# Handing the loads of a memory-bound attention kernel from SyncE's hardware queue to Pool's software queue, with 8 rows asked for per packet

## The chip, the cores and the metric

The kernel runs on one core of one Trainium2 chip. The metric is device time in microseconds (us). Times are medians of several executions. "Landing" is the moment at which the last of 16 semaphore writes of a load has happened, by the packet records of the trace. A "row" is the part of a load in one partition. The profile calls SyncE's queue `hardware_dynamic` and Pool's `software_dynamic`; here they are the hardware and the software queue, and the "hardware descriptors" and "software descriptors" are loads by the one and by the other. The experiments ran in three sessions, each on another chip and each with the kernel before in the same rounds.

## The reference

One query token attends over a cache of 16384 keys and values in 32 heads; the result is projected and mixed, by a gate, with a small gated MLP of the same token.

```
q      = (x @ wq).reshape(1, 1, 32, 128)                    # x: 512
scores = einsum('bhqd,bhkd->bhqk', q, k_cache) * 128**-0.5  # k_cache: 32 x 16384 x 128, bf16
o      = einsum('bhqk,bhkd->bhqd', softmax(scores), v_cache)
a      = o.reshape(1, 1, 4096) @ wo
b      = gMLP(x)                                            # small
out    = g * a + (1 - g) * b
```

The two caches are 268 MB of the 279.58 MB that must be read, and every byte is used once.

## The kernel before

Heads are worked in 16 pairs. A pair has one load of keys (K_i) and one of values (V_i), 8.4 MB each: 128 partitions of 64 KB. In the packet records a load is 16 chains of 8 rows of 64 KB, each chain ended by one semaphore write: so each of the 16 DMA engines carries 8 rows of every load. Three buffers of 64 KB per partition take the loads in turn, in the order K_0, K_1, V_0, K_2, V_1, K_3, ... A load waits until the load three places before it has been used. SyncE issues all loads; Pool waits for each landing and hands it on to DVE or PE.

```python
k_at = [max(2 * i - 1, 0) for i in range(NP)]            # place of K_i in the order of loads
v_at = [min(2 * i + 2, 2 * NP - 1) for i in range(NP)]
# ... (user[n]: the event after which the buffer of load n is free)
for n, kind, i in loads:
    wait = [user[n - 3]] if n >= 3 else [w_free] if buf[n % 3] is setup else []
    src = (k_src if kind == "k" else v_src)[i]
    cuts, sems = (0, KP), [(ld_k if kind == "k" else ld_v)[i % 2]]
    # ... (the last pair's loads are cut into pieces)
    for a, b, done in zip(cuts[:-1], cuts[1:], sems):
        sp.op(lambda e, a=a, b=b, n=n, src=src: e.dma_start(
            out=buf[n % 3][:, a * Dh:b * Dh], in_=src[:, a * Dh:b * Dh]),
            wait=wait if a == 0 else (), inc=(done, 16))
# ... (five pieces of wo, the same way)

def hand(e, loaded, to, n):
    e.wait_ge(loaded, 16).then_inc(to, n)
    e.nop().then_inc(loaded, -16)
# ... (pool_pairs: a hand() for every load, in order)
```

K_1 (load 1) waits for nothing and is queued right behind K_0. V_0 (load 2) needs the buffer that holds the weights of the setup; it waits for `w_free`, the end of the gMLP. DVE multiplies the keys by the query, PE sums the products and ACT takes the exponentials, after which a key buffer is free. V_1 is load 4: it waits until K_1 (load 1) has been used.

The softmax here doesn't subtract the row's maximum and nothing guards it: scores larger than these inputs give would overflow.

Of the kernel before, what the change touches and what calls it, by code (L numbers as in the profile page):

```python
# [13 lines left out]
Dh = 128  # L14
H = 32
NP = H // 2
D = 512
# [9 lines left out]
KP = Sk // 64  # L27
# [7 lines left out]
WG = 8  # L35
NT = NG // TG
ZB = F // 4
K_CUTS = (0, 128, 256)
V_CUTS = (0, 160, 224, 256)
WO_CUTS = (0, 16, 24, 28, 31, 32)  # L40
WIDE = 24
# [126 lines left out]
def gated_mix_kernel(nc, A_x, A_k_cache, A_v_cache, A_wq, A_wo, B_x, B_w_in, B_w_sp, B_b_sp,  # L168
                     B_w_out, gate_w, out):
    def sb(name, shape, dt):  # L170
# [3 lines left out]
    buf = [bufs[:, b * ROW:(b + 1) * ROW] for b in range(3)]  # L174
# [42 lines left out]
    wo_at = 2 * NP  # L217
# [5 lines left out]
    wo = buf[wo_at % 3]  # L223
# [5 lines left out]
    sem = nc.alloc_semaphore  # L229
# [1 line left out]
    half = sem("half")  # L231
    ld_x, ld_g, ld_q, ld_w, ld_u, st_out = (
        sem(n) for n in ("ld_x", "ld_g", "ld_q", "ld_w", "ld_u", "st_out"))
    ld_k = [sem(f"ld_k{b}") for b in range(2)]
    ld_v = [sem(f"ld_v{b}") for b in range(2)]
    ld_kh = [sem(f"ld_kh{b}") for b in range(len(K_CUTS) - 1)]
    ld_vp = [sem(f"ld_vp{b}") for b in range(len(V_CUTS) - 1)]
    ld_o = [sem(f"ld_o{b}") for b in range(len(WO_CUTS) - 1)]
    k_s, v_s, mul_s, red_s, sum_s, exp_s, sl_s, pv_s, drn_s, zer_s, wo_s = (
        sem(n) for n in ("k_s", "v_s", "mul_s", "red_s", "sum_s", "exp_s", "sl_s", "pv_s", "drn_s",  # L240
                         "zer_s", "wo_s"))
# [4 lines left out]
    pool, sp, pe, dve, act = (Queue(nc, e, n) for e, n in (  # L246
        (nc.gpsimd, "pool"), (nc.sync, "sp"), (nc.tensor, "pe"), (nc.vector, "dve"),
        (nc.scalar, "act")))
# [6 lines left out]
    def value(e, reg, top):  # L255
# [5 lines left out]
        out=ident[:, :], in_=ident[:, :], compare_op=ALU.not_equal, fill=1.0, base=0,  # L261
        pattern=[[-1, P]], channel_multiplier=1))
    for t in [L_sb, p_t, zero]:
# [5 lines left out]
           inc=(ld_x, 16))  # L269
    act.op(lambda e: e.dma_start(out=gw_row[:, :], in_=gate_w.rearrange("(a d) -> a d", a=1)),  # L270
           inc=(ld_g, 16))
    act.op(lambda e: e.dma_start(out=wb_row[:, 0:1], in_=B_w_sp), inc=(ld_g, 16))
    act.op(lambda e: e.dma_start(out=wb_row[:, 1:2], in_=B_b_sp.rearrange("(a d) -> a d", a=1)),
           inc=(ld_g, 16))
    sp.op(lambda e: e.dma_start(out=wq, in_=A_wq.rearrange("(p c) n -> p (c n)", c=DC)),
          inc=(ld_q, 16))
    sp.op(lambda e: e.dma_start(out=w_in, in_=B_w_in.rearrange("(p c) f -> p (c f)", c=DC)),
          inc=(ld_w, 16))
    sp.op(lambda e: e.dma_start(out=w_out, in_=B_w_out.rearrange("(p k) n -> p (k n)", k=FhC)),
          inc=(ld_u, 16))  # L280

    for c in range(DC):
# [9 lines left out]
        out=sel[:, :].rearrange("h (i x) -> h i x", x=P + 1)[:, :, 0:P:4],  # L292
        in_=ident[0:H, 0:H].unsqueeze(1).broadcast_to([H, 4, H])), wait=[const_ok, ident_ok],
        mark=True)
    dve.op(lambda e: e.tensor_reduce(
        out=pick[:, :].rearrange("p (r s) -> p s r", r=4),
        in_=ident[:, :].rearrange("p (g x) -> p x g", x=32)[:, 0:8, :]
# [10 lines left out]
           wait=[g_ok], mark=True)  # L308
# [52 lines left out]
    for h in range(2):  # L361
        zh = ps_all[:, 6 * h * 512:(6 * h + 2) * 512].rearrange("p (b x) -> p b x", b=2)[:, :, 0:ZB]
        dve.op(lambda e, h=h, zh=zh: e.tensor_tensor(  # L363
            out=zm[:, 2 * h * ZB:2 * (h + 1) * ZB].rearrange("p (b m k) -> p b m k", b=2, k=FhC),
# [5 lines left out]
        out=z[:, :].rearrange("p (e k) -> p e k", e=2),  # L370
        in_=zm.rearrange("p (e m k) -> p e k m", e=2, k=FhC), axis=AX.X, op=ALU.add))
    dve.chain(lambda e: e.scalar_tensor_tensor(
        out=zt[:, :], in0=z[:, :], scalar=0.044715, in1=z[:, :], op0=ALU.mult, op1=ALU.mult))
    zt_ok = dve.chain(lambda e: e.scalar_tensor_tensor(
        out=zt[:, :], in0=zt[:, :], scalar=1.0, in1=z[:, :], op0=ALU.add, op1=ALU.mult))
# [5 lines left out]
           wait=[sg_ok], mark=True)  # L381
# [11 lines left out]
        out=var[:, :], in0=mv[:, 0:1], scalar=mv[:, 0:1], in1=mv[:, 1:2], op0=ALU.mult,  # L393
# [9 lines left out]
        out=u[:, :], in0=z2n[:, :], scalar=gm_sb[:, 0:1], in1=z[:, 0:FhC], op0=ALU.mult,  # L403
        op1=ALU.mult))
    u_ok = (dve.sem, dve.n)
# [6 lines left out]
        out=ps_all[:, 2 * 512:6 * 512].rearrange("p (n s x) -> p n s x", n=2, s=2)[:, :, 0, :],  # L412
        in_=zero[:, :].unsqueeze(1).broadcast_to([P, 2, 512])))
# [188 lines left out]
    user = {}  # L602
    for i in range(NP):
        user[k_at[i]], user[v_at[i]] = used_k[i], used_v[i]
    loads = sorted([(n, "k", i) for i, n in enumerate(k_at)]
                   + [(n, "v", i) for i, n in enumerate(v_at)])
    for n, kind, i in loads:
        wait = [user[n - 3]] if n >= 3 else [w_free] if buf[n % 3] is setup else []
        src = (k_src if kind == "k" else v_src)[i]
        cuts, sems = (0, KP), [(ld_k if kind == "k" else ld_v)[i % 2]]  # L610
        if i == NP - 1:
            cuts, sems = (K_CUTS, ld_kh) if kind == "k" else (V_CUTS, ld_vp)
        for a, b, done in zip(cuts[:-1], cuts[1:], sems):
            sp.op(lambda e, a=a, b=b, n=n, src=src: e.dma_start(
                out=buf[n % 3][:, a * Dh:b * Dh], in_=src[:, a * Dh:b * Dh]),
                wait=wait if a == 0 else (), inc=(done, 16))
    wo_src = A_wo.rearrange("(p k) n -> p (k n)", k=H)
    for j, (a, b) in enumerate(zip(WO_CUTS[:-1], WO_CUTS[1:])):
        sp.op(lambda e, a=a, b=b: e.dma_start(out=wo[:, a * D:b * D], in_=wo_src[:, a * D:b * D]),  # L619
              wait=[user[wo_at - 3]] if a == 0 else (), inc=(ld_o[j], 16))  # L620

    def hand(e, loaded, to, n):
        e.wait_ge(loaded, 16).then_inc(to, n)
        e.nop().then_inc(loaded, -16)

    def pool_pairs(e):
        hand(e, ld_k[0], k_s, 2)
        with e.Fori(0, NP // 2 - 1):
            hand(e, ld_k[1], k_s, 2)
            hand(e, ld_v[0], v_s, NT)  # L630
            hand(e, ld_k[0], k_s, 2)
            hand(e, ld_v[1], v_s, NT)
        for j in range(len(ld_kh)):
            hand(e, ld_kh[j], k_s, 1)
        hand(e, ld_v[0], v_s, NT)
        for j, (a, b) in enumerate(zip(V_CUTS[:-1], V_CUTS[1:])):
            hand(e, ld_vp[j], v_s, (b - a) * NT // KP)

    pool.raw(pool_pairs)

    dve.op(lambda e: e.reciprocal(out=rl[:, :], in_=l_ps[:, 0:H]), wait=[(sl_s, 1)], mark=True)  # L641
    dve.chain(lambda e: e.tensor_scalar(out=rl[:, :], in0=rl[:, :], scalar1=g_sb[:, 0:1],
# [12 lines left out]
    o2_ok = dve.op(lambda e: e.tensor_copy(out=o2[:, :], in_=l_ps[:, P:P + H]), wait=[o2p_ok],  # L655
                   mark=True)

    def pool_wo(e):
        e.wait_ge(*d_zero)
        e.wait_ge(*o2_ok)  # L660
        for j, (a, b) in enumerate(zip(WO_CUTS[:-1], WO_CUTS[1:])):
            if a < WIDE:
                hand(e, ld_o[j], wo_s, (min(b, WIDE) - a) // WG)

    pool.raw(pool_wo)

    def pe_wide(e):
        va, pa = (counter(e, n, 0) for n in ("wa", "oa"))
# [33 lines left out]
    for q in (dve, act):  # L702
        mine = range(NC)[:NC // 2] if q is dve else range(NC)[NC // 2:]
        for s in mine:
            ok = q.op(lambda e, s=s, copy=(q is act): (e.copy if copy else e.tensor_copy)(  # L705
                out=res[0:1, s * DQ:(s + 1) * DQ], in_=a_ps[32 * s:32 * s + 1, 0:DQ]),
                wait=[y_ok] if s in mine[:1] else (), mark=(s == mine[-1]))
        sp.raw(lambda e, ok=ok: e.wait_ge(*ok))
    sp.op(lambda e: e.dma_start(out=out.rearrange("a b d -> (a b) d"), in_=res[:, :]),
          inc=(st_out, 16))  # L710
# [19 lines left out]
def build(inputs):  # L730
    import numpy as _np
    import concourse.bacc as _bacc
    from concourse import mybir as _mybir

    nc = _bacc.Bacc("TRN2", target_bir_lowering=False, num_devices=1, dynamic_dma_scratch_size=4096)
    arrays, args = {}, []
    for name in _INS:
        a = _np.ascontiguousarray(inputs[name])
        if a.dtype.kind in "iu":
            a = a.astype(_np.int64)  # L740
        arrays[f"in_{name}_dram"] = a
        args.append(nc.dram_tensor(f"in_{name}_dram", a.shape, _mybir.dt.from_np(a.dtype), kind="ExternalInput").ap())
    for i, (shape, dtype) in enumerate(_OUTS):
        dt = _mybir.dt.from_np(_np.dtype(dtype))
        args.append(nc.dram_tensor(f"out_{i}_dram", shape, dt, kind="ExternalOutput").ap())
    gated_mix_kernel(nc, *args)
    return nc, arrays
# [9 lines left out]
```

## Time and profile before

| | before |
|---|---|
| median time | 651.7 us (20 runs, 651.5 to 652.7) |
| span in the profile | 650.0 us |
| DMA, mean over the span | 430 GB/s |
| PE, DVE busy | 66%, 52% |
| mean step from landing to landing, steady state | 19.350 us |

These are lines of the profile's page of the kernel before. `DMA` gives the busy share of the 16 DMA engines in tenths for 40 equal slices, `GB/s` what they moved; the line starting `DMA 4%` is the chain that ended last.

```profile
span 650.0 us, 7735 instructions
DMA  9999999999999999999999989999999999999998
DMA packets 6203, 279.60 MB, mean 430 GB/s; under 512 B 695, under 2 KB 826, under 8 KB 1210
q1 hardware_dynamic: 6194, 279.58, 99.6%
DMA 4%; PE 0%; SPq 0%; issue 0%; DVE 0%; ACT 0%; ACTq 0%
```

The loads bound the kernel from end to end: the packets of the hardware queue take 99.6% of the span of the 16 engines. How little is left is told by the packet records: the fastest rows of 64 KB start 2414 ns apart on an engine, and 99% of the rows that follow another without a gap (under 2500 ns from start to start) start 2414 to 2429 ns after it. An estimate from the 2414 ns, if all 279.58 MB moved at that rate on 16 engines, is 643.6 us for the bytes.

The timeline of SyncE before shows when (start and duration of the issuing instruction):

```profile
2.03 1.04 SPq L614 DMA_DIRECT2D bufs<-in_A_k_cache_dram  x2
35.15 0.33 SPq L614 DMA_DIRECT2D bufs<-in_A_v_cache_dram  x1
66.40 0.33 SPq L614 DMA_DIRECT2D bufs<-in_A_k_cache_dram  x1
91.86 0.33 SPq L614 DMA_DIRECT2D bufs<-in_A_v_cache_dram  x1
101.32 0.33 SPq L614 DMA_DIRECT2D bufs<-in_A_k_cache_dram  x1
```

In order they are K_0 and K_1, V_0, K_2, V_1, K_3. By the packet records K_2 ends at 95.05 us on the first engine and 95.59 on the last. The lead, from V_1's issue to the end of K_2 on the first engine, is 3.2 us. Compute decides when V_1 can be issued, and in the timeline of DVE compute begins when K_0 has landed (37.56 us) and has been handed on:

```profile
31.06 0.23 DVE L402 SCALAR_TENSOR_TENSOR u<-z2n,gm_sb,z 128x7 bf16<-128x7 f32 x1
38.32 8.76 DVE L557 TENSOR_TENSOR bufs<-bufs,qb  x2 [7.03 <-DVEq L84]
```

The first line is the event `u_ok` (31.3 us), which the change uses. The second is the first product with K_0.

### The profile page before, as it was taken

How to read it: one execution, taken by the hardware profiler on the slowest of the kernel's cores; microseconds unless marked ns; L12 is line 12 of the kernel's file. 1: busy time of each engine (PE TensorE's matmuls, PEld its weight loads, DVE VectorE, ACT ScalarE, POOL GpSimd, SP SyncE). 2: the span in 40 equal slices, each digit the busy share in tenths (PEclk: the TensorE clock that was granted, in tenths of full speed). 3: DMA queues.
4: the chain of work that ended last, by engine and by line, in shares of the span. 5: the costliest groups of instructions: out<-in, count | busy, mean ns of one | idle time of the engine just before them, and what ended most of it. 6: DMA issues, size and time to landing. Idle time of an engine off the chain costs nothing. (4 is left out here: it accounts for less than half of the span.)

```text
span 650.0 us, 7735 instructions
## 1 busy us (share of the span) xinstructions
PE 428.8 (66%) x2464; PEld 44.2 (7%) x1304; DVE 336.2 (52%) x159; ACT 45.8 (7%) x112; POOL 2.1 (0%) x10
## 2 busy tenths in 40 slices
PE   0547687847487584747857476684747757478767
PEld 0000000000101000010000101000010100001012
DVE  3457848256380745618265470835629075465600
ACT  2200100000001000010100001000010100001011
POOL 1000000000000000000000000000000000000000
PEclk9958788969779686987968798686988968798999
DMA  9999999999999999999999989999999999999998
GB/s 385 466 415 452 452 391 448 452 432 407 452 452 399 440 452 444 395 452 452 407 432 452 452 387 452 452 407 432 452 452 391 448 452 423 415 425 478 390 428 345
DMA packets 6203, 279.60 MB, mean 430 GB/s; under 512 B 695, under 2 KB 826, under 8 KB 1210
## 3 DMA queue, kind: packets, MB, share of 16 engines
q1 hardware_dynamic: 6194, 279.58, 99.6%
q8 instruction: 1, 0.02, 0.0%
q10 hardware_dynamic: 8, 0.00, 0.0%
HBM read 279.58 MB, written 0.00 MB: 430 GB/s over the span
## 5 line engine op out<-in xcount | busy, mean ns | idle before, releaser
L557 DVE TENSOR_TENSOR bufs<-bufs,qb x64 | 281.5, 4419 | 167.7 <-DVEq L84 167.7
L88 PE MATMUL ps_all<-bufs,ident 128*128 x960 | 267.6, 436 | 0.0
L475 PE MATMUL ps_all<-bufs,ident 128*128 x64 | 28.6, 446 | 148.2 <-PEq L84 148.2
L101 PE MATMUL ps_all<-bufs,p_t 128*8 x1024 | 79.1, 384 | 30.5 <-PEq L84 19.9
L542 DVE TENSOR_REDUCE s_sb<-ps_all 128x64 f32<-128x512 f32 x64 | 44.1, 689 | 97.8 <-DVEq L84 97.8
L88 PE MATMUL ps_all<-zero,ident 128*8 128x512 bf16 (+1 forms) x165 | 57.9, 383 | 0.0
L569 ACT ACTIVATE p_t<-s_sb 64x256 f32 (+1 forms) x32 | 13.3, 414 | 433.4 <-ACTq L84 433.0
L475 PEld LDWEIGHTS ps_all<-bufs,ident 128*128 128x128 bf16 x64 | 6.3, 99 | 367.8 <-issue 367.8
L101 PEld LDWEIGHTS ps_all<-bufs,p_t 128*8 x1024 | 17.9, 82 | 163.6 <-issue 163.2
L510 PE MATMUL ps_all<-pick,d_sb 128*128 128x2 f32 x128 | 16.8, 253 | 16.5 <-PEq L84 16.5
L510 PEld LDWEIGHTS ps_all<-pick,d_sb 128*128 128x128 f32 x128 | 15.5, 191 | 34.7 <-issue 34.7
L578 ACT COPY d_sb<-ps_all 128x512 f32<-128x512 f32 x16 | 9.4, 585 | 104.3 <-ACTq L84 104.3
L583 ACT CAST ps_all<-zero 128x512 f32<-128x512 bf16 x15 | 8.8, 589 | 1.7
L644 DVE TENSOR_TENSOR o_sb<-ps_all,rl 128x32 bf16<-128x32 f32 x1 | 0.2, 191 | 11.5 <-PE ps_all L510 11.5
L641 DVE RECIPROCAL rl<-ps_all 128x32 f32<-128x32 f32 x1 | 0.4, 357 | 11.1 <-PE ps_all L531 11.1
L363 DVE TENSOR_TENSOR bufs<-ps_all,ident 128x896 f32<-128x896 f32 x2 | 2.1, 1086 | 7.6 <-PE ps_all L88 7.6
L569 ACT ACTIVATION_READ_ACCUMULATOR p_t<-s_sb (+1 forms) x32 | 5.9, 185 | 0.0
L305 PE MATMUL ps_all<-xgw,const-float32-1.0 1*128 1x3 f32 x2 | 0.6, 360 | 8.0 <-DVE xgw L302 8.0
L101 PE MATMUL ps_all<-bufs,u 128*1 x14 | 2.6, 372 | 3.3 <-ACT ps_all L409 2.5
L88 PE MATMUL ps_all<-bufs,xb 128*128 x12 | 4.2, 476 | 0.0
L328 PE MATMUL ps_all<-bufs,xb 128*128 x4 | 2.1, 517 | 3.2 <-DMA bufs<-in_B_w_in_dram 3.2
L101 PE MATMUL ps_all<-bufs,xb 128*64 x32 | 3.6, 381 | 0.0
(76 smaller groups left out, 38.2 us busy)
## 6 DMA issues: line engine op xcount, KB each, us to landing
bufs<-in_A_k_cache_dram SPq DMA_DIRECT2D x2, 4096.0 KB, 35.5
bufs<-in_A_v_cache_dram SPq DMA_DIRECT2D x1, 5120.0 KB, 33.8
bufs<-in_A_wq_dram SPq DMA_DIRECT2D x1, 4096.0 KB, 12.2
bufs<-in_A_v_cache_dram SPq DMA_DIRECT2D x1, 2048.0 KB, 38.4
bufs<-in_A_wo_dram SPq DMA_DIRECT2D x1, 2048.0 KB, 24.4
bufs<-in_B_w_in_dram SPq DMA_DIRECT2D x1, 1792.0 KB, 15.4
bufs<-in_A_v_cache_dram SPq DMA_DIRECT2D x1, 1024.0 KB, 40.4
bufs<-in_A_wo_dram SPq DMA_DIRECT2D x1, 1024.0 KB, 26.5
```

The costliest lines, as they stand in the source:

```text
L88: ins = eng.matmul(out, lhsT=lhsT, rhs=rhs, **flags).ins
L101: ins = eng.matmul(bank[0:m, 0:n], lhsT=lhsT, rhs=rhs, **flags).ins
L305: g_ok = pe.op(lambda e: e.matmul(g_ps, lhsT=ones_f[0:1, :], rhs=xgw[:, :], start=True, stop=True), wait=[xgw_ok], mark=True)
L328: if n else matmul_on(nc, e, lambda: e.matmul(args[0], lhsT=args[1], rhs=args[2], **flags), [at, (xa, 0)]))
L363: dve.op(lambda e, h=h, zh=zh: e.tensor_tensor(out=zm[:, 2 * h * ZB:2 * (h + 1) * ZB].rearrange("p (b m k) -> p b m k", b=2, k=FhC), in0=z ...
L475: matmul_on(nc, e, lambda: e.matmul(s3, lhsT=ident[:, :], rhs=k3[:, :, 0:W], start=True, **flags), [(kw, 0)])
L510: ins = e.matmul(o2, lhsT=d_sb[:, r * Dh:(r + 1) * Dh], rhs=pick[:, r * 2:(r + 1) * 2], start=False, stop=False, skip_group_check=True)
L542: return e.tensor_reduce(out=s_sb[:, c * QK:(c + 1) * QK], in_=s_ps[c % 2].rearrange("p (j w) -> p j w", w=W), axis=AX.X, op=ALU.add)
L557: e.tensor_tensor(out=k3, in0=k3, in1=qi, op=ALU.mult).then_inc(mul_s, 1)
L569: e.activation(out=p_t[rows, bass.ds(at, NG * 8)].rearrange("p (t c) -> p t c", c=8)[:, :, 4 * s:4 * s + 4], in_=s_sb[rows, :].rearrange(" ...
L578: return e.copy(out=d_sb[:, :], in_=d_ps)
L583: e.copy(out=d_ps, in_=zero[:, :]).then_inc(drn_s, 1)
```

## The change: intent and diff

The intent is fewer packet boundaries: Pool's loads ask that an engine's 8 rows go as one packet (`single_packet`). To use that, Pool issues all loads from K_1 on. SyncE keeps the setup loads and K_0, and takes over handing landings on. K_1 keeps one row to a packet and waits for `u_ok`, because the two queues now share the engines.

```diff
     for n, kind, i in loads:
         wait = [user[n - 3]] if n >= 3 else [w_free] if buf[n % 3] is setup else []
         src = (k_src if kind == "k" else v_src)[i]
+        if n == 0:
+            sp.op(lambda e, src=src: e.dma_start(out=buf[0], in_=src), inc=(ld_kf, 16))
+            landed[kind, i] = [((ld_kf, 16), 2)]
+            continue
 ...
-            sp.op(lambda e, a=a, b=b, n=n, src=src: e.dma_start(
-                out=buf[n % 3][:, a * Dh:b * Dh], in_=src[:, a * Dh:b * Dh]),
-                wait=wait if a == 0 else (), inc=(done, 16))
+            pool.op(lambda e, a=a, b=b, n=n, src=src: e.dma_start(
+                out=buf[n % 3][:, a * Dh:b * Dh], in_=src[:, a * Dh:b * Dh], single_packet=n > 1),
+                wait=(wait if a == 0 else ()) if n > 1 else [u_ok], inc=(done, 16))
 ...   (wo: sp.op -> pool.op with single_packet=True)
-    pool.raw(pool_pairs)
+    for n, kind, i in loads:
+        for done, units in landed[kind, i]:
+            sp.raw(lambda e, done=done, units=units, to=(k_s if kind == "k" else v_s):
+                   e.wait_ge(*done).then_inc(to, units))
```

More of the change, by code (lines that the diff above doesn't have):

```diff
@@ L233, in gated_mix_kernel @@
         sem(n) for n in ("ld_x", "ld_g", "ld_q", "ld_w", "ld_u", "st_out"))
-    ld_k = [sem(f"ld_k{b}") for b in range(2)]
-    ld_v = [sem(f"ld_v{b}") for b in range(2)]
+    ld_kf = sem("ld_kf")
+    ld_b = [sem(f"ld_b{b}") for b in range(3)]
     ld_kh = [sem(f"ld_kh{b}") for b in range(len(K_CUTS) - 1)]
@@ L606, in gated_mix_kernel @@
                    + [(n, "v", i) for i, n in enumerate(v_at)])
+    landed = {}
     for n, kind, i in loads:
@@ L609, in gated_mix_kernel @@
         src = (k_src if kind == "k" else v_src)[i]
-        cuts, sems = (0, KP), [(ld_k if kind == "k" else ld_v)[i % 2]]
+        if n == 0:
+            sp.op(lambda e, src=src: e.dma_start(out=buf[0], in_=src), inc=(ld_kf, 16))
+            landed[kind, i] = [((ld_kf, 16), 2)]
+            continue
+        cuts, sems, whole = (0, KP), [ld_b[n % 3]], (n - 1) // 3 * 16 + 16 if n % 3 else n // 3 * 16
         if i == NP - 1:
-            cuts, sems = (K_CUTS, ld_kh) if kind == "k" else (V_CUTS, ld_vp)
+            cuts, sems, whole = (*((K_CUTS, ld_kh) if kind == "k" else (V_CUTS, ld_vp)), 16)
@@ L613, in gated_mix_kernel @@
+        landed[kind, i] = []
         for a, b, done in zip(cuts[:-1], cuts[1:], sems):
-            sp.op(lambda e, a=a, b=b, n=n, src=src: e.dma_start(
-                out=buf[n % 3][:, a * Dh:b * Dh], in_=src[:, a * Dh:b * Dh]),
-                wait=wait if a == 0 else (), inc=(done, 16))
+            pool.op(lambda e, a=a, b=b, n=n, src=src: e.dma_start(
+                out=buf[n % 3][:, a * Dh:b * Dh], in_=src[:, a * Dh:b * Dh], single_packet=n > 1),
+                wait=(wait if a == 0 else ()) if n > 1 else [u_ok], inc=(done, 16))
+            landed[kind, i].append(((done, whole), (b - a) * NT // KP if kind == "v" else
+                                    2 // (len(cuts) - 1)))
@@ L617, in gated_mix_kernel @@
     wo_src = A_wo.rearrange("(p k) n -> p (k n)", k=H)
     for j, (a, b) in enumerate(zip(WO_CUTS[:-1], WO_CUTS[1:])):
-        sp.op(lambda e, a=a, b=b: e.dma_start(out=wo[:, a * D:b * D], in_=wo_src[:, a * D:b * D]),
-              wait=[user[wo_at - 3]] if a == 0 else (), inc=(ld_o[j], 16))
-    def hand(e, loaded, to, n):
-        e.wait_ge(loaded, 16).then_inc(to, n)
-        e.nop().then_inc(loaded, -16)
-    def pool_pairs(e):
-        hand(e, ld_k[0], k_s, 2)
-        with e.Fori(0, NP // 2 - 1):
-            hand(e, ld_k[1], k_s, 2)
-            hand(e, ld_v[0], v_s, NT)
-            hand(e, ld_k[0], k_s, 2)
-            hand(e, ld_v[1], v_s, NT)
-        for j in range(len(ld_kh)):
-            hand(e, ld_kh[j], k_s, 1)
-        hand(e, ld_v[0], v_s, NT)
-        for j, (a, b) in enumerate(zip(V_CUTS[:-1], V_CUTS[1:])):
-            hand(e, ld_vp[j], v_s, (b - a) * NT // KP)
@@ L639, in gated_mix_kernel @@
-    pool.raw(pool_pairs)
+        pool.op(lambda e, a=a, b=b: e.dma_start(out=wo[:, a * D:b * D], in_=wo_src[:, a * D:b * D],
+                                                single_packet=True),
+                wait=[user[wo_at - 3]] if a == 0 else (), inc=(ld_o[j], 16))
+    for n, kind, i in loads:
+        for done, units in landed[kind, i]:
+            sp.raw(lambda e, done=done, units=units, to=(k_s if kind == "k" else v_s):
+                   e.wait_ge(*done).then_inc(to, units))
     dve.op(lambda e: e.reciprocal(out=rl[:, :], in_=l_ps[:, 0:H]), wait=[(sl_s, 1)], mark=True)
@@ L656, in gated_mix_kernel, with hand_wo @@
                    mark=True)
-    def pool_wo(e):
+    def hand_wo(e):
         e.wait_ge(*d_zero)
@@ L662, in pool_wo @@
             if a < WIDE:
-                hand(e, ld_o[j], wo_s, (min(b, WIDE) - a) // WG)
-    pool.raw(pool_wo)
+                e.wait_ge(ld_o[j], 16).then_inc(wo_s, (min(b, WIDE) - a) // WG)
+    sp.raw(hand_wo)
     def pe_wide(e):
```

## The prediction

> **What bounds the kernel now.** The loads. On the profile's page the 16 DMA engines are at nine tenths or more in all 40 slices; SyncE's queue takes 99.6% of their span and 279.58 MB moved in 650.0 us (430 GB/s). PE is 66% busy, DVE 52%. The chain of waits ends in a DMA (4.2%), only 2.2 us before the store. [...]a 64 KB row is one packet, 3840 of them, mean 2421 ns, starting 2414 to 2427 ns apart on an engine[...]. Any packing can win little.
>
> **Removed.** 7 of 8 packet boundaries of each load from V_0 on. An engine has some 240 packets[...]. I expect 1.3 us.
>
> **Added.** [...]In steady state a load is issued 11 to 21 us before the load ahead ends (issue to landing 30.9 and 40.9 us, a load 19.35), so this is hidden. Hand-overs by SyncE cost as Pool's.
>
> **Not hidden: the start.** K_1 now waits for u_ok (31.3 us in the timeline) and comes by another queue while K_0 runs until 37.56 (packet 6 starts at 32.2 to 32.7, packet 7 at 34.6 to 35.1). [...]K_0 lands one packet, 2.4 us, later (4.8 if K_1 is ready before 32.2). That loses no bandwidth, but compute starts later: DVE's first product moves from 38.3 to 40.7, K_1's exponentials from 91.86 to 94.3, and V_1 is issued then. K_2's last bytes come at 95.0 to 95.6, so the queue runs dry there for 0 to 1 us, once. Then compute gains 3 us a pair and the margin returns.
>
> **Sum.** 651.7 - 1.3 + 0.4 = 650.8; I say 650.7 us, range 648.6 to 653.5. Faster by over 2%: 0.01, within: 0.96, slower: 0.03.
>
> **Right or wrong, by the profile.** (1) Packets fall from 6203 to 1000 to 1500, data packets of 512 KB near 19.3 us. (2) Load to load falls from 19.35 to 19.28 us[...]. (3) DVE's first product at 40 to 41 us. (4) A DMA gap under 1.5 us near 95 us, none elsewhere. (5) The chain still ends in the load of wo; PE and DVE busy times unchanged.
>
> **What would make it wrong.** Software descriptors that feed some engines more slowly: a load ends with its slowest engine, and 2% is 13 us. [...]K_1 taking two packets in turn, or an 8-row packet moving at another rate than 8 packets.

The sum was 651.7 - 1.3 + 0.4 = 650.8 us, given as 650.7. The 1.3, and the 19.28 us that goes with it, are to be read as my guesses (that packing could win little is borne by the estimate of 643.6 us above); the 0.4 is what was put on the dry spell near 95 us. Two statements are to be set beside the traces: the page shows two of the 40 slices at 8 tenths, not at 9; and the hand-over, from K_0's landing to DVE's first product, took 0.76 us through Pool before (37.56 to 38.32) and 0.72 through SyncE after (42.53 to 43.25).

## The result, and the profile after

The median is 653.52 us (10 runs, 652.31 to 655.36) against 651.7 before, where a gain of 1.0 us was forecast. The ratio is 1.0031 (95% interval 1.0022 to 1.0039): a loss of about 1.8 us, within 2%, and just outside the predicted range (648.6 to 653.5). Ratios here and below are the mean time of one kernel's runs over that of the other's in the same rounds, so they are not quite the ratio of the medians quoted. The profiled run took 654.58 us. The runs also scatter more: 3 us where before it was 1.2.

The page after:

```profile
span 653.2 us, 7683 instructions
DMA  9999989999999999999999999999999999999998
DMA packets 6043, 279.60 MB, mean 428 GB/s; under 512 B 695, under 2 KB 698, under 8 KB 1050
q0 software_dynamic: 5456, 264.24, 93.7%
q1 hardware_dynamic: 578, 15.34, 5.5%
DMA 4%; PE 0%; POOL 0%; issue 0%; DVE 0%; ACT 0%; ACTq 0%
```

Two things are to be read. The number of packets hardly moved, and the records still show rows of 65536 B: 3712 on the software queue. The fall by 160 is in the last pieces of wo alone: 128 rows of 1 KB have become 32 records of 4 KB, and 128 of 3 KB 64 records of 6 KB. So a record can hold several rows, and none holds two rows of 64 KB. And one slice, the sixth (82 to 98 us), fell from 9 to 8. Cutting the span in two (columns: window, its length, busy time of PE, PEld, DVE, ACT and Pool, granted clock, DMA share, GB/s) puts the loss at the start. First before, then after:

```profile
0.00:100.00 100.00, 56.46 (x272) 4.59 (x106) 57.42 (x42) 13.04 (x24) 2.15 (x10) 0.85 1.00 427
100.00:600.00 500.00, 336.10 (x1914) 32.80 (x997) 265.91 (x106) 28.43 (x78) 0.00 (x0) 0.83 1.00 434
```

```profile
0.00:100.00 100.00, 51.19 (x243) 4.18 (x82) 57.28 (x42) 11.87 (x22) 4.41 (x14) 0.85 0.97 416
100.00:600.00 500.00, 331.12 (x1936) 33.37 (x1020) 264.06 (x106) 29.62 (x80) 14.31 (x27) 0.85 1.00 433
```

After 100 us the rates are 434 and 433 GB/s. Before 100 us, 11 of 427 GB/s are missing, which over 100 us is 2.6 us. The timeline of Pool after shows the same five issues as those of SyncE above, less K_0:

```profile
31.35 0.68 POOL L620 DMA_DIRECT2D bufs<-in_A_k_cache_dram  x1 [28.10 <-DVE u L402]
35.18 0.54 POOL L620 DMA_DIRECT2D bufs<-in_A_v_cache_dram  x1 [3.15 <-PE ps_all L101]
72.22 0.53 POOL L620 DMA_DIRECT2D bufs<-in_A_k_cache_dram  x1 [36.50 <-ACT p_t L569]
96.31 0.53 POOL L620 DMA_DIRECT2D bufs<-in_A_v_cache_dram  x1 [23.56 <-ACT p_t L569]
105.87 0.53 POOL L620 DMA_DIRECT2D bufs<-in_A_k_cache_dram  x1 [9.03 <-PE ps_all L510]
```

K_2 is issued at 72.22 in place of 66.40, V_1 at 96.31 in place of 91.86. And in the timeline of DVE the first product starts 4.9 us later:

```profile
43.25 4.42 DVE L557 TENSOR_TENSOR bufs<-bufs,qb  x1 [12.21 <-DVEq L84]
```

The packet records of the trace say why. They carry the queue, start, duration and size of every row, but not the engine; a row is put on an engine by its start, which follows the end of a row before it. This is a table made from them, not a view of the page:

```
K_0's last rows, on the engine that was last (us)        | on 14 of the 16 engines
32.86-35.28 K_0 row 6     hardware queue                 | 34.57-37.43  K_0 row 7
35.28-37.70 K_1 row 0     software queue, goes first     | 36.98-39.84  K_1 row 0
37.69-40.11 K_0 row 7                                    | 39.40-39.85  K_0's semaphore write
40.11-42.52 K_1 row 1     goes first again               |
42.53       K_0's semaphore write: only now K_0 "landed" |

             K_2 ends on the 16 engines   V_1 issued   V_1's first rows   step to V_1's landing
before       95.05 to 95.59               91.86        95.05 to 95.59     19.35
after        95.14 to 95.73               96.31        97.55 to 98.39     22.45
```

The sixteenth engine was as the 14, 0.3 us later: but for the one engine of the left column, K_0 would have landed at 40.13. From 95.73 to 97.55 us no engine moved anything, the last engine began 0.85 us later still, and V_1's first rows took 2.65 to 3.26 us in place of 2.42. V_1 landed 3.1 us later than a step of 19.35 after K_2, and the profiled run is 3.0 us slower than the time of the undisturbed kernels (651.6). So the lost time is the late start of this one load; the question for the chip is whether that chain of causes holds, which part of the change starts it, and where the saving from the packing is.

### The profile page after: what moved, and what is told of

The parts are those of the page before. It is cut to its first block, busy times and chain, and to the rows that moved or that the text cites. A ratio compares the mean times of both kernels' runs of the same rounds, so it can differ in the third digit from the quotient of the medians.

```text
span 653.2 us, 7683 instructions
## 1 busy us (share of the span) xinstructions
PE 421.4 (65%) x2464; PEld 44.5 (7%) x1304; DVE 335.9 (51%) x159; ACT 45.8 (7%) x112; POOL 22.9 (4%) x49
## 2 busy tenths in 40 slices
DMA packets 6043, 279.60 MB, mean 428 GB/s; under 512 B 695, under 2 KB 698, under 8 KB 1050
## 5 line engine op out<-in xcount | busy, mean ns | idle before, releaser
L88 PE MATMUL ps_all<-bufs,ident 128*128 x960 | 259.9, 425 | 0.0
L475 PE MATMUL ps_all<-bufs,ident 128*128 x64 | 28.3, 442 | 158.4 <-PEq L84 158.2
L620 POOL DMA_DIRECT2D bufs<-in_A_v_cache_dram x18 | 9.5, 530 | 400.7 <-ACT p_t L569 388.8
L620 POOL DMA_DIRECT2D bufs<-in_A_k_cache_dram x16 | 8.6, 540 | 179.5 <-PE ps_all L510 105.5
L88 PE MATMUL ps_all<-bufs,xb 128*128 x12 | 4.0, 455 | 0.0
```

The costliest lines, as they stand in the source:

```text
L88: ins = eng.matmul(out, lhsT=lhsT, rhs=rhs, **flags).ins
L475: matmul_on(nc, e, lambda: e.matmul(s3, lhsT=ident[:, :], rhs=k3[:, :, 0:W], start=True, **flags), [(kw, 0)])
L620: pool.op(lambda e, a=a, b=b, n=n, src=src: e.dma_start(out=buf[n % 3][:, a * Dh:b * Dh], in_=src[:, a * Dh:b * Dh], single_packet=n > 1), ...
```

## The experiments

The theory, START: K_1 in a second queue takes turns with the end of K_0, K_0's completion is late, compute is late, V_1 is issued too late, and the engines run dry once. Rivals: STEADY or SOFTWARE (Pool's queue or the packing cost something in every load; in experiments 5, 7 and 8, that turns do not matter and K_0 is late only where and because K_1 comes by Pool's queue), and PACKING PAYS (the saving is there but covered). Each ratio below is to the kernel before, run in the same rounds.

### 1. Packing undone (e1_rows)

```diff
-                out=..., in_=..., single_packet=n > 1),
+                out=..., in_=..., single_packet=False),      # and the same for wo
```

> The changed kernel with one row to a packet everywhere: Pool still issues the same loads at the same places, only the packing of 8 rows into one packet is undone. Theory START (the loss is all at the start: K_1 in a second queue delays K_0's completion, compute starts 4.9 us later, V_1 is issued after K_2 has ended and the DMA engines stand dry for about 2.5 us near 96 us; packing saves nothing): 653.5 us plus or minus 0.7, the same gap near 96 us, and 19.35 us from landing to landing as in the changed kernel. Rival PACKING PAYS (my prediction: 8 rows in a packet save 1.3 to 2 us, hidden by a larger loss elsewhere): 655 us or more, and 19.35 us where the changed kernel has 19.28. Rival PACKING COSTS (a packet of 512 KB moves worse): 651.7 or less.

Measured: 653.67 us (652.91 to 654.25), ratio 1.0029. Steady step 19.344 us, with packing 19.345, before 19.350. PACKING PAYS is out at the size I predicted, and PACKING COSTS too. In sizes and numbers the packet records are those of the changed kernel: undoing the flag undid nothing that the trace shows, and the rows of 1 and 3 KB were joined without it too. The gap was there but smaller in the profiled execution: K_1 was issued at 32.93, 1.6 us later than in the changed kernel, and no engine let it in before K_0's row 7. K_0 landed at 40.08, V_1 was issued at 94.67, and its landing came 1.25 us late (that run took 652.91 us):

```profile
94.67 0.53 POOL L620 DMA_DIRECT2D bufs<-in_A_v_cache_dram  x1 [24.95 <-ACT p_t L569]
```

### 2. K_1 issued after w_free (e2_wfree)

```diff
-                wait=(wait if a == 0 else ()) if n > 1 else [u_ok], inc=(done, 16))
+                wait=(wait if a == 0 else ()) if n > 1 else [w_free], inc=(done, 16))
```

> The changed kernel with one word changed: Pool issues K_1 after w_free (35.2 us) in place of u_ok (31.3 us), so that it is ready after K_0 has ended at 37.6 us. In the changed kernel 3.6 us passed from K_1's wait to its first packets. Theory START: K_0 completes at 37.6 us as in the kernel before, DVE's first product is back at 38.3 us, V_1 is issued at about 92 us and the gap near 96 us is gone; in its place the engines stand dry 1 to 1.5 us at 37.6 us if the 3.6 us hold again. Time 652.0 to 653.0. Rival STEADY (software descriptors or the packing cost something in every load, the start matters little): 653.3 to 653.8, as the changed kernel.

Measured: 653.82 us, ratio 1.0028. The expected time (652.0 to 653.0) was missed, though the events were as START says: K_0 landed at 37.65, DVE started at 38.38, V_1 was issued at 92.02 and the gap near 96 us was gone. K_1 was issued at 35.40:

```profile
35.40 0.68 POOL L620 DMA_DIRECT2D bufs<-in_A_k_cache_dram  x1 [32.17 <-PE ps_all L101]
92.02 0.53 POOL L620 DMA_DIRECT2D bufs<-in_A_v_cache_dram  x1 [24.88 <-ACT p_t L569]
```

By the time alone this is STEADY's figure; the steady step of 19.345 us, no longer than before, rules a cost in every load out. (The 3.6 us of the expectation are 3.9 by the packet records: 31.35 to 35.28.) Fourteen engines went on to it without a gap between 37.12 and 37.64, but two got its first row only at 39.03 and 39.42. On the fourteen, the first row took 2.6 to 3.2 us in place of 2.42. The two never caught up: from then on each load's first and last engine ended 2.6 us apart (0.5 us before the gap). Averaged over 16 engines only 0.26 us of idle time stood near 38 us, yet K_1 landed 2.6 us late and this execution took 654.27 us. The time is set by the worst engine, because each engine carries its own 8 rows of every load (16 chains of 8 in the records).

### 3. Late compute alone, in the kernel before (e3_late5)

```diff
 def pool_pairs(e):
+    e.wait_ge(ld_k[0], 16)
+    for j in range(8):
+        e.memset(pad[:, :], 0.0).then_inc(late, 1)
+        e.wait_ge(late, j + 1)
     hand(e, ld_k[0], k_s, 2)
```

> The kernel before, all loads from SyncE's hardware queue, one change: Pool runs 8 dummy fills (about 5 us) between K_0's landing and its hand-over to DVE. No second queue and no software descriptors. Theory START: the 5 us move DVE's first product to about 43.3 us, V_1 is issued at about 96.8 us, K_2 has ended at 95.6 us, so the engines stand dry for 2 to 3 us near 96 us and the time is 653.8 to 655, that is the whole loss of the changed kernel without anything of its change. Rival STEADY: late compute at the start is made up later (the page shows PE and DVE idle a third or more), so 651.7 to 652.2.

Measured: 654.86 us, ratio 1.0052. Lines of the timelines of Pool and SyncE of this run (the dummy fills, and V_1's issue):

```profile
38.23 4.60 POOL L631 MEMSET pad<- 128x512 bf16 x8 [34.99 <-DMA bufs<-in_A_k_cache_dram]
...
95.28 0.33 SPq L616 DMA_DIRECT2D bufs<-in_A_v_cache_dram  x1
```

With one queue, the hardware one, and no packing, 4.6 us of delay before the hand-over brought V_1 to 95.28 and lost 3.0 us. So late compute at the start is enough for the loss; STEADY, which held that it would be made up, is out. Of the loss 1.8 us is V_1's landing; another 0.6 us is in two later loads (steps of 19.75 and 19.56 us) and is not explained. A further 0.6 us lies outside the profile's span: the time is 2.0 us above the span in all five runs of this kernel, and mostly 1.4 in the runs of the kernel before. That is not explained either. After the dry spell V_1's first rows took up to 3.3 us, most of them over 2.7, in place of 2.42.

### 4. Compute made early, in the changed kernel (e4_halves)

```diff
-            sp.op(lambda e, src=src: e.dma_start(out=buf[0], in_=src), inc=(ld_kf, 16))
-            landed[kind, i] = [((ld_kf, 16), 2)]
+            for ca, cb, done in zip(K_CUTS[:-1], K_CUTS[1:], ld_kf):       # two halves of 4 MB
+                sp.op(... buf[0][:, ca * Dh:cb * Dh] ..., inc=(done, 16))
+            landed[kind, i] = [((done, 16), 1) for done in ld_kf]
```

> The changed kernel, with K_0 loaded by SyncE in two halves of 4 MB, each with its own semaphore, so that DVE can start on the first half at about 31 to 33 us. K_1 still comes by Pool's queue at u_ok and still takes turns with K_0's second half. Theory START: the completion of K_0's second half is still late (40 to 42.5 us), but compute is no longer late, V_1 is issued before 92 us, no gap near 96 us, and the time is 651.2 to 651.9, as the kernel before. Rival STEADY: the gap was not the cause of most of the loss; 653 or more. Rival PACKING PAYS: 650.5 or less, since the gap is gone and the saving is left.

Measured: 651.68 us (651.67 to 651.89), ratio 0.9997. In the timelines of DVE and Pool the first product starts on the first half at 31.73, the second half is still late (landed at 42.57, product at 43.26), yet V_1 is issued at 85.40:

```profile
31.73 8.76 DVE L557 TENSOR_TENSOR bufs<-bufs,qb  x2 [0.42 <-DVEq L84]
43.26 4.43 DVE L557 TENSOR_TENSOR bufs<-bufs,qb  x1
85.40 0.53 POOL L622 DMA_DIRECT2D bufs<-in_A_v_cache_dram  x1 [24.81 <-ACT p_t L569]
```

The software queue, the packing and the collision with K_0 are all still there, and the whole loss and the whole scatter are gone. With experiment 3 this shows START: late compute is enough for the loss, and without it there is none.

### 5. A second hardware queue (e5_actq)

The kernel before, with K_1 and V_0 issued by ScalarE's hardware queue:

```diff
+    act.op(lambda e: e.dma_start(out=buf[1], in_=k_src[1]), wait=[u_ok], inc=(ld_k[1], 16))
 ...
+    act.op(lambda e: e.dma_start(out=buf[2], in_=v_src[0]), wait=[w_free], inc=(ld_v[0], 16))
 ...
     for n, kind, i in loads:
+        if n in (1, 2):
+            continue
```

> The kernel before with hardware descriptors throughout; K_1 and V_0 alone are issued from ScalarE's hardware queue, K_1 at u_ok as in the change, the rest from SyncE's. A second queue without software descriptors and without packing. Theory TURNS (the second queue alone makes K_0 late[...]): K_1 is ready about 1.3 us after 31.3 us, so on all 16 engines it takes a turn before K_0's packet 7 and one before K_0's semaphore write: K_0 completes at about 42.4 us (before: 37.6; the changed kernel 42.5), DVE starts at 43 us, the engines stand dry for 2 to 3 us near 96 us, time 653.5 to 655. Rival SOFTWARE[...]: K_0 completes at 37.6 to 40 us and the time is 651.7 to 652.3.

Measured: 653.49 us, ratio 1.0025; the profiled run 654.23. K_1's issue by ScalarE and DVE's first product in the timelines:

```profile
31.00 0.37 ACTq L410 DMA_DIRECT2D bufs<-in_A_k_cache_dram  x1
...
43.10 8.76 DVE L559 TENSOR_TENSOR bufs<-bufs,qb  x2 [12.13 <-DVEq L84]
```

K_1's first rows came 3.6 us or more after its issue, not the 1.3 us that I expected (near the 1.24 us from V_1's issue to its first row after the change, on a dry engine), so K_1 got in before K_0's row 7 on 10 of 16 engines, not on all. One is enough: K_0 landed at 42.35. V_1 was issued at 95.99, all engines were dry for 1.3 us from 95.61, and V_1 landed 2.6 us late (I had expected a dry spell of 2 to 3 us; the time is at the lower edge of what I expected). The second queue alone gives the loss, with no load by the software queue; SOFTWARE is not needed.

### 6. The software queue used once before K_1 (e6_warm_wfree)

The kernel of experiment 2, with a 1 KB load by Pool at the start (its result is not used):

```diff
+    pool.op(lambda e: e.dma_start(out=gw_too[:, :], in_=gate_w.rearrange("(a d) -> a d", a=1)),
+            inc=(ld_p, 16))
 ...
-                wait=(wait if a == 0 else ()) if n > 1 else [w_free], inc=(done, 16))
+                wait=(wait if a == 0 else ()) if n > 1 else [(ld_p, 16), w_free], inc=(done, 16))
```

> The changed kernel with K_1 at w_free as in e2_wfree, and one tiny load (1 KB, not used) issued by Pool at about 3 us, so that K_1 is not the first load of the software queue. In e2_wfree 14 engines went on to K_1 without a gap, and two stood dry for 1.9 and 2.3 us and stayed that late to the end of the kernel, which is the whole of its 2.0 us loss. If the late two come from the first use of the queue, this one has no gap at 37.6 us and no gap near 96 us, and the time is 651.6 to 652.2. [...]the gap stays on some engines and the time is 652.5 to 654.

Measured: 653.74 us, ratio 1.0027. K_1 was issued at 36.11, and its first rows started at 37.44 to 38.86, 1.3 to 2.75 us after; most engines had a gap, and K_1 landed 1.9 us late.

```profile
36.11 0.56 POOL L624 DMA_DIRECT2D bufs<-in_A_k_cache_dram  x1 [32.29 <-PE ps_all L101]
```

That is the second outcome of the expectation (652.5 to 654). The gap stays when the queue has been used before, so first use is not the whole cause. A part of it is not excluded: K_1 was issued 0.7 us later here than in experiment 2, and its slowest first row still came sooner after the issue (2.75 us against 4.0).

### 7. K_1 asked for as one packet too (e9_onepacket)

```diff
-                out=..., in_=..., single_packet=n > 1),
+                out=..., in_=..., single_packet=True),
```

> The changed kernel with K_1, too, in packets of 8 rows (512 KB, 19.3 us on an engine). Theory TURNS: [...]K_0 completes at about 56.5 us if no engine lets K_1 in before K_0's packet 7, or at about 76 us if one does[...]. DVE's first product starts at 57 or 76.5 us, K_2 and V_1 are issued as much later, the engines stand dry for some 17 us in all (or some 36 us), time about 669 (or 688) us. Rival SOFTWARE: turns do not matter, 653 to 655 us.

Measured: 654.34 us (653.77 to 654.84), ratio 1.0039. My expectation of some 669 us failed. No engine let K_1 in before K_0's row 7 here, and then K_0's semaphore write came after one row of K_1 (39.53 to 39.99 us), not after eight. The first product in DVE's timeline:

```profile
40.73 8.76 DVE L557 TENSOR_TENSOR bufs<-bufs,qb  x2 [9.04 <-DVEq L84]
```

So what delays K_0 is one row of 64 KB (2.42 us), whatever packing is asked for. The step that failed, my assumption that K_1's 8 rows would go ahead in one piece, was not shown by any run. The records show single rows of 64 KB here as in all other runs, and no packet of 8 rows. The loss has the usual cause: V_1 was issued at 93.33, the last engine was dry until 97.4, and V_1 landed 2.2 us late.

### 8. K_1 in rows of a quarter (e9_quarters)

```diff
+        if n == 1:
+            cuts, sems = (0, 64, 128, 192, 256), [ld_b[1]] * 4
 ...   (K_1 is handed on at a count of 64; later counts of that semaphore grow by 48)
```

> The changed kernel with K_1 issued as four loads of 16 KB rows at the same place, so that a turn of K_1 is 16 KB (0.62 us) in place of 64 KB (2.42 us). Theory TURNS: two turns delay K_0 by about 1.2 us at most, K_0 completes at 38.2 to 38.8 us, DVE starts at 39 to 39.6 us, V_1 is issued before 93.3 us, the gap near 96 us is under 0.2 us, and the time is 651.7 to 652.2 us. Rival SOFTWARE: 653 to 654 us as the changed kernel.

Measured: 652.36 us, ratio 1.0011 (0.9997 to 1.0024), the profiled run 652.36. The timelines of DVE and Pool:

```profile
39.15 8.76 DVE L557 TENSOR_TENSOR bufs<-bufs,qb  x2 [6.52 <-DVEq L84]
...
91.63 0.53 POOL L624 DMA_DIRECT2D bufs<-in_A_v_cache_dram  x1 [24.49 <-ACT p_t L569]
```

K_0 landed at 38.43, 0.9 us late in place of 2.4 to 5.0, and there was no gap near 96 us. K_1 was issued at 32.94 and no engine let it in before K_0's row 7, so this is to be compared with 2.4. The delay shrinks with the row (16 KB rows took 0.61 us, the median in the trace of the kernel before, in place of 2.42), as the theory of turns by rows says. The time was 0.16 us above what I expected: K_1 landed at 57.38, 0.5 us later than before, 0.25 us of which was there at the setup loads already. Another 0.5 us lies outside the span: the time is 1.9 us above the span here, where it is mostly 1.4 before.

### 9. Half the delay (e7_late2)

Experiment 3 with `range(4)` in place of `range(8)`.

> The kernel before with 4 dummy fills on Pool (2.3 us) between K_0's landing and its hand-over, where e3_late5 had 8 (4.6 us) and lost 3.0 us. In e3_late5 V_1 was issued at 95.3 us and its first bytes came 1.0 to 2.3 us later, while K_2's engines ended at 95.2 to 95.8. Theory START has a threshold: here V_1 is issued at about 93 us, its bytes are ready at 94 to 95.3, before the engines run dry, so hardly anything is lost: 651.7 to 652.3 us, gap under 0.3 us. Rival PROPORTIONAL (each us of late compute costs time by itself): 653.2 us or so.

Measured: 653.65 us, ratio 1.0032: not the 651.7 to 652.3 of my theory, and by the time alone the rival's figure. The trace shows how. V_1 was issued at 93.41:

```profile
93.41 0.33 SPq L616 DMA_DIRECT2D bufs<-in_A_v_cache_dram  x1
```

Fourteen engines went on to V_1 without a gap, the first at 95.06, 1.65 us after the issue. Two got its first row at 96.67 and 96.85, 3.3 us or more after the issue, and these first rows took 2.92 and 3.19 us. V_1 landed 1.83 us late (step 21.18), and to the end of the kernel the first and last engine ended 2.4 to 2.5 us apart. PROPORTIONAL is no better: experiment 3, with twice the delay, had V_1 just as late (1.78). So the loss does not grow in step with the delay, but the 1 to 2 us of lead of my theory were too few: with 3.2 us before nothing was lost, with 1.65 here and 1.8 in experiment 7 V_1 landed 1.83 and 2.16 us late. The averaged idle time near 96 us is only 0.16 us here; the mean over engines hides the loss.

### 10. Controls without the gap (e8_before_halves, e10_halves_packed, e10_halves_rows)

The kernel before with K_0 in two halves; the kernel of experiment 4 again; and that kernel with `single_packet=False` everywhere. All on one chip in the same rounds.

> Control for e4_halves: the kernel before, hardware descriptors, with K_0 in two halves. If halving K_0 were worth something by itself, e4_halves would hide a loss of the change. Expected: 651.4 to 651.9 us, as the kernel before (651.85) and as e4_halves (651.68). If it is under 651.2, the software queue does cost something in e4_halves.

> e4_halves again, on the same chip as the next kernel: the changed kernel with K_0 in two halves, 8 rows to a packet. 651.5 to 651.9 us, five runs within 0.3 us.

> e4_halves with one row to a packet: the packing alone undone, where no gap and no scatter cover it. If packing saves nothing (theory now: rows start 2414 ns apart with and without it[...]): the same time as e10_halves_packed within 0.2 us. If packing saves what I predicted: 1.3 us or more slower than it.

Measured: 651.72, 651.70 and 651.65 us, ratios 1.0003, 1.0001 and 1.0002; the ranges are 651.56 to 651.87, 651.62 to 651.73 and 651.57 to 651.82. Hardware or software queue, 8 rows or 1 asked for per packet: no difference of the medians above 0.1 us. The saving of 1.3 us that I forecast would be a ratio of 0.998, below the 95% interval of the packed kernel (0.9988 to 1.0015). In sizes and numbers the packet records of the last two kernels are the same, so what is shown to save nothing is the asking for packets of 8 rows; no trace shows that such packets were formed.

### All gaps at V_1 together

This table is made from the timelines and packet records of the profiled runs. "Late" is the step from K_2's landing to V_1's less 19.35 us.

| run | V_1 issued | K_2 ends, first to last engine | late | time of this run |
|---|---|---|---|---|
| before | 91.86 | 95.05 to 95.59 | 0.00 | 651.47 |
| e7_late2 | 93.41 | 95.06 to 95.79 | 1.83 | 653.48 |
| e9_onepacket | 93.33 | 95.14 to 95.61 | 2.16 | 653.88 |
| e1_rows | 94.67 | 95.51 to 95.91 | 1.25 | 652.91 |
| e3_late5 | 95.28 | 95.23 to 95.78 | 1.78 | 654.46 |
| e5_actq | 95.99 | 95.09 to 95.61 | 2.59 | 654.23 |
| after | 96.31 | 95.14 to 95.73 | 3.10 | 654.58 |
| e4_halves | 85.40 | 95.33 to 95.78 | 0.00 | 651.67 |

Five of the six late runs lie 1.3 to 3.0 us above 651.6, within 0.15 us of their "late"; e3_late5 has 1.1 us more, of which 0.6 is the two slow loads named there and the rest lies outside the span. No version beat the kernel before: those without a gap tie with it. That is what a kernel within 1.3% of 643.6 us leaves, the estimate from rows that start 2414 ns apart.

## Why the prediction was wrong

- **The bound and the place of the risk were right.** The loads bound the kernel, steady state is unaffected (433 against 434 GB/s), and the only dry spell came near 95 us, by the chain predicted: K_0 late, DVE's first product late, V_1 late. What was wrong is both terms of the sum, 0.4 us lost and 1.3 us saved.
- **"K_0 lands one packet, 2.4 us, later" was mis-sized.** It landed 5.0 us later (42.53 against 37.56) in the profiled run. I forgot that K_0's semaphore write, too, comes only after a row of K_1 (its data ended at 40.11, the write at 42.53), so an engine that lets K_1 in before row 7 loses two rows, 4.8 us. My own "4.8 if K_1 is ready before 32.2" named the size but tied it to the wrong time: K_1's row was ready at 35.28 and still got in on one engine, which was enough. In e1_rows no engine did, and K_0 was 2.5 us late. That this is the 2.4 of the forecast is luck: I had a row of K_1 go before K_0's row 7, and there it went only before the semaphore writes.
- **The guess of the time from an issue to the first bytes was too low.** No trace had given it. K_1's first row started 3.9 us after its issue began (the engines that were free up to 35.02 took K_0's row 7 instead), and V_1's 1.24 to 2.1 us after on dry engines. By the hardware queue V_1's came 1.0 to 2.3 us after its issue on dry engines (e3_late5), and 3.3 us or more after on two of 16 (e7_late2). By that figure the 3.2 us of lead in the kernel before left no slack; that is an estimate, no run tried leads between 1.8 and 3.2 us.
- **"The queue runs dry for 0 to 1 us, once; +0.4 us" was the term that broke the sum.** In the profiled run it was 3.1 us, with V_1 issued at 96.31 and not at 94.3; in e1_rows, with V_1 at 94.67, still 1.25. I counted a mean; the loss is that of the worst engine, and it was not made up to the end of the kernel (e2_wfree, e7_late2: engines 2.6 and 2.4 to 2.5 us apart), because every engine has the same share of every load, 8 rows.
- **"I expect 1.3 us" saved by the packing was wrong: it is 0.** The step that failed is "7 of 8 packet boundaries of each load" removed: the records show the same single rows of 64 KB with 8 rows asked for per packet and without, and at best they start 2414 ns apart either way. What a boundary costs at 64 KB is therefore not measured, and the cost of a packet that I had reckoned with was not shown. What the rows take beyond 2414 ns is scatter, 0 to 15 ns a row for 99% of the rows that follow without a gap before the change and for 97% after it.
- Point (1) of what should show, fewer packets and records of 512 KB, was wrong: 6043 packets and none over 64 KB, though the records do join the small rows of wo. Point (2), a step of 19.28 us, was wrong: 19.345 against 19.350. Point (3), DVE's first product at 40 to 41 us, was wrong (43.25), and so was point (4), a gap under 1.5 us. Point (5) held: the chain ends in wo, and DVE's busy time is the same; PE's fell from 428.8 to 421.4 us, which is off the critical path.
- Pool was not held up while DVE multiplied: its issues of K_2 and V_1 took 0.53 us each; that of K_2, at 72.22, fell into two products of DVE that ran from 70.18 for 8.76 us.

What stays open: why just two engines of 16 get a new load's first row so late (e2_wfree, e7_late2), and why K_0's semaphore write comes only after a row of K_1: in the run after the change 2.4 us after the end of K_0's data on all 16 engines (40.11 to 42.53 on the last). That packets of 8 rows were formed is shown by no record.

## What to carry to other kernels

In a kernel bound by loads, ask first for each load how long before the end of the load ahead it is issued; here 3.2 us was enough and 1.8 us was not, and one missed lead cost the worst engine's gap for good (in e7_late2 the engines ended 2.4 to 2.5 us apart to the end of the kernel). Moving loads to a second queue while the first is still busy delayed the first queue's last load here by a row of the second (2.4 us), and its semaphore write by one row more. And look whether the records change when a flag asks for packing, before a saving is booked: here they did not. When means over engines show nothing, look at the spread between the first and last engine's end of a load: in e7_late2 it went from 0.7 to 2.5 us where the averaged idle time was 0.16 us.
